# Where the weight blocks are fetched, where the first tile's FFN is placed, and which engine clears and multiplies at the start of a fused GateLoop and maxout-FFN kernel

## The chip, the cores and the metric

The kernel runs on one core of a Trainium2 chip. The metric is the device time in microseconds (us) of one execution. Five engines work side by side: TensorE (PE in the profile; PEld is its weight load), VectorE (DVE), ScalarE (ACT), GpSimd (POOL) and SyncE (SP), which issues transfers. The span that a trace shows (from the first to the last instruction) is about 1.8 us shorter than the time of the same execution.

## The reference

The reference is a gated linear recurrence over 768 steps (batch 4, 8 heads of 48), followed by a feed-forward block on its output:

```python
mag = np.sqrt(a_re * a_re + a_im * a_im)
scale = np.minimum(mag, 0.999) / (mag + 1e-06)
a_re_n, a_im_n = (a_re * scale, a_im * scale)
for t in range(S):                      # S = 768
    new_re = ar * S_re - ai * S_im      # ar, ai: the gates of step t
    new_im = ar * S_im + ai * S_re
    kv = np.einsum('bhd,bhe->bhde', k[:, :, t], v[:, :, t])
    S_re, S_im = (new_re + kv, new_im)
    y[:, :, t] = np.einsum('bhd,bhde->bhe', q[:, :, t], S_re)
# x = y as 3072 tokens x 384
h = np.maximum(np.maximum(x @ w1, x @ w2), x @ w3)     # w1..w3: 384 x 768
out = h @ w_out                                        # w_out: 768 x 384
```

The weights are made as `np.random.randn(...) * (1.0 / np.sqrt(n))` and arrive as float64, so the kernel must turn them into float32 on the chip. Everything else is float32.

## The kernel before

The 3072 tokens are 24 tiles of 128; two tiles are a group that shares one pass of gate work (logarithms, angles, products), so there are twelve groups. A tile goes through its gates, a Q and K preparation, the recurrence in chunked form, then nine "up" steps (three column blocks by w1, w2, w3, with a maximum on VectorE) and one "out" step (`op`) of the FFN. The up steps need the rounded w1 to w3, the out step needs all of w_out.

The twelve weight blocks of 768 KB are rounded like this; each takes five operations on VectorE and two on ScalarE:

```python
def load_weight(dst, src, i):
    ...
    if i % 3 == 2:
        raw = wo...                     # part of a weight tile not yet in use
    else:
        raw = fp2.tile([P, n, m, 2], I32, tag="hT", name="raw")
    nc.sync.dma_start(out=raw..., in_=src.bitcast(I32))
    low, high = raw[:, :, :, 0].bitcast(U32), raw[:, :, :, 1]
    ex = fp2.tile([P, n, m], I32, tag="xT", name="ex")
    nc.vector.tensor_scalar(out=ex, in0=high, scalar1=0x7FF00000, scalar2=None, op0=OP.bitwise_and)
    nc.scalar.activation(out=ex, in_=ex, func=AF.Relu, scale=8.0, bias=wbias)
    nc.vector.scalar_tensor_tensor(out=ex, in0=high, scalar=-0x80000000, in1=ex,
                                   op0=OP.bitwise_and, op1=OP.bitwise_or)
    nc.vector.tensor_scalar(out=high, in0=high, scalar1=0x000FFFFF, scalar2=None, op0=OP.bitwise_and)
    nc.scalar.activation(out=dst, in_=high, func=AF.Copy, scale=2.0 ** -20, bias=1.0)
    nc.vector.scalar_tensor_tensor(out=dst, in0=low, scalar=2.0 ** -52, in1=dst, op0=OP.mult, op1=OP.add)
    nc.vector.tensor_tensor(out=dst, in0=dst, in1=ex.bitcast(FP), op=OP.mult)
```

The multiplies that GpSimd takes over from VectorE (`ai` by `L` in the gates, `k` and `q` by `E` in the products) are chosen by group:

```python
(nc.gpsimd if g > 0 else nc.vector).tensor_tensor(out=ai, in0=ai, in1=L, op=OP.mult)
...
eng = nc.gpsimd if g > 0 else nc.vector
eng.tensor_tensor(out=hd(T[nm, x]), in0=E, in1=hd(T[nm, x]), op=OP.mult)
```

And the order of the program; `weave` spreads several lists of steps over the given shares of one another:

```python
load(0)                                 # all of group 0's inputs, then
load_v(0)
constants_early()
for t in us["k"] + us["q"] + fs + gs + vbs[2:]:
    nc.gpsimd.memset(t, 0.0)            # whole tiles, on GpSimd
weights = weight_steps()
...                                     # gates of group 0
for f in weights[:3]:                   # the first three blocks, fetched and rounded here
    f()
load(1)
angles(0, list(range(C)))
...
for g in range(NG):
    load_v(g + 1)
    load(g + 2)
    if g == 0:
        weave((0.0, 1.0, loop_steps(0)), (0.0, 0.7, weights[3:]),
              (0.15, 0.58, pre_steps(1)), (0.7, 1.0, ffn_steps([0])))
    else:
        ...
```

## Time and profile before

| | before |
|---|---|
| time, median of the first 3 runs | 751.53 us (751.1 to 753.01) |
| span of the profiled execution | 748.2 us |
| end of the last multiply that rounds weights ("T") | 123.24 us |
| TensorE busy / idle up to T | 59.79 / 63.45 us |
| TensorE busy / idle after T | 611.13 / 13.83 us |

The page gives the busy share of 40 slices in tenths; the table of stretches gives exact busy time between two chosen moments; the waits say who sat idle for whom; the timeline lists single instructions with start and duration. One more piece of the timeline of VectorE before the first cumulative sum (columns: start, duration, engine, line, operation, output<-inputs, size):

```profile
28.42 0.95 DVE L345 TENSOR_TENSOR w<-w,ar 128x768 f32<-128x768 f32 x1
29.29 1.82 DVE L281 SCALAR_TENSOR_TENSOR w<-raw,w 128x768 f32<-128x768 uint32 x2
31.03 1.82 DVE L282 TENSOR_TENSOR w<-w,ex 128x768 f32<-128x768 f32 x2
32.77 0.56 DVE L274 TENSOR_SCALAR ex<-wo 128x768 int32<-128x768 int32 x1
33.23 0.95 DVE L346 TENSOR_TENSOR w<-w,ai 128x768 f32<-128x768 f32 x1
```

L345 and L346 are the two angle operations that the cumulative sum needs.

### The profile page before, as it was taken

Reading aid. Unit: us, or ns where it says so; the run is one execution under the profiler, and the core shown is the slowest. Engines: PE = TensorE matmul, PEld = TensorE weight load, DVE = VectorE, ACT = ScalarE, POOL = GpSimd, SP = SyncE. Lnnn points to the kernel's source line nnn. Section 1 sums busy time; section 2 is a strip of 40 time slices with the busy share of each in tenths; the row PEclk is TensorE's granted clock in tenths of the full one; section 3 lists DMA queues with packets and bytes.
Section 4 is the critical chain, followed back from the end, with each engine's and each line's share of the span. In section 5 each row is a group of like instructions: output and inputs, shape, how many; then the busy total and the mean of one; then the engine's idle time right before and its main releaser. Section 6 shows DMA issues by size and latency. Waiting matters only on the chain.

```text
span 748.2 us, 17645 instructions
## 1 busy us (share of the span) xinstructions
PE 670.9 (90%) x7620; PEld 543.1 (73%) x7620; DVE 518.4 (69%) x706; ACT 402.2 (54%) x677; POOL 130.4 (17%) x133
## 2 busy tenths in 40 slices
PE   1166279989999999999999999999999999999998
PEld 0054168968778878878878868878878878788785
DVE  4889997787866866866856867867857767655210
ACT  7595565666647546556556556556566465322010
POOL 9302400411302203102103103103004005000000
PEclk9986699999999999999999999999999999999999
DMA  9764430050220320320320420410410210000000
GB/s 173 156 178 136 121 92 23 8 103 10 54 65 11 56 66 9 74 51 7 72 54 6 77 52 5 91 35 7 91 33 10 46 33 2 1 23 2 12 11 22
DMA packets 134158, 38.91 MB, mean 52 GB/s; under 512 B 126784, under 2 KB 129856, under 8 KB 134080
## 3 DMA queue, kind: packets, MB, share of 16 engines
q1 hardware_dynamic: 133824, 37.76, 22.8%
q8 instruction: 60, 0.98, 0.6%
q14 instruction: 18, 0.15, 0.1%
q10 hardware_dynamic: 256, 0.01, 0.0%
HBM read 33.03 MB, written 4.72 MB: 50 GB/s over the span
## 4 chain that ended last, share of the span: by engine, by line
PE 73%; issue 11%; DVE 7%; ACT 4%; POOL 2%; SPq 2%; DMA 1%; ACTq 0%; POOLq 0%; DVEq 0%
PE up L575 35%; PE op L586 12%; PE tp L432 5%; PE dk L529 4%; PE B L492 4%; PE y L557 3%; PE A L492 2%; PE mds L395 2%; PE sfx L395 2%; PE F L445 2%; PE cs L350 2%; ACT e L106 1%; DVE QB L459 1%; SPq L226 1%; POOL ai L328 1%
## 5 line engine op out<-in xcount | busy, mean ns | idle before, releaser
L575 PE MATMUL up<-xT,w 128*128 128x256 f32 (+1 forms) x1404 | 299.3, 367 | 6.5 <-ACT xT L563 6.2
L575 PEld LDWEIGHTS up<-xT,w 128*128 128x128 f32 x1404 | 249.0, 191 | 46.4 <-ACT xT L563 7.7
L328 POOL TENSOR_TENSOR ai<-ai,L 128x768 f32<-128x768 f32 x11 | 30.4, 2759 | 418.4 <-ACT L L106 314.1
L586 PE MATMUL op<-wo,hT 128*128 128x384 f32 x288 | 97.9, 490 | 0.0
L580 DVE TENSOR_TENSOR hT<-hT,up 128x512 f32<-128x512 f32 (+1 forms) x78 | 49.9, 640 | 40.0 <-PE up L575 39.8
L586 PEld LDWEIGHTS op<-wo,hT 128*128 128x128 f32 x288 | 52.9, 190 | 33.3 <-DVE hT L580 0.5
L459 DVE TENSOR_TENSOR Q<-Q,f 112x512 f32<-112x512 f32 x48 | 40.3, 840 | 44.9 <-ACT f L106 44.9
L434 ACT COPY K<-tp 112x512 f32<-112x512 f32 x48 | 27.9, 581 | 60.0 <-PE tp L432 59.8
L578 ACT COPY hT<-up 128x512 f32<-128x512 f32 (+1 forms) x39 | 21.3, 548 | 69.6 <-PE up L575 68.6
L588 ACT COPY ot<-op 128x384 f32<-128x384 f32 x24 | 11.5, 477 | 81.5 <-PE op L586 81.5
L541 DVE TENSOR_TENSOR g<-g,dk 112x384 f32<-112x384 f32 x40 | 22.1, 552 | 47.0 <-PE dk L529 46.4
L350 PE MATMUL cs<-w,upto 128*128 128x384 f32 x48 | 20.5, 555 | 34.5 <-DVE w L346 34.5
L529 PEld LDWEIGHTS dk<-vb,uk 128*112 128x112 f32 x384 | 42.7, 183 | 9.9 <-issue 5.5
L557 PEld LDWEIGHTS y<-atm,vb 128*32 128x32 f32 x1536 | 39.7, 112 | 13.5 <-issue 8.4
L529 PE MATMUL dk<-vb,uk 128*112 128x96 f32 x384 | 43.1, 267 | 6.0 <-issue 5.2
L557 PE MATMUL y<-atm,vb 128*32 128x64 f32 x1536 | 47.1, 224 | 0.4 <-DVE atm L510 0.4
L557 PE MATMUL y<-QG,g 112*32 112x64 f32 x1536 | 46.5, 222 | 0.0
L459 DVE TENSOR_TENSOR QB<-Q,f 112x512 f32<-112x512 f32 (+1 forms) x48 | 46.3, 999 | 0.0
L405 POOL TENSOR_TENSOR k<-E,k 128x384 f32<-128x384 f32 x22 | 30.2, 1372 | 68.9 <-ACT E L106 65.2
L492 PE MATMUL A<-Q,K 112*64 112x96 f32 x768 | 38.7, 254 | 3.7 <-DVE Q L459 3.1
L492 PEld LDWEIGHTS A<-Q,K 112*64 112x64 f32 x768 | 33.9, 140 | 9.4 <-issue 5.2
L106 ACT ACTIVATE f<-F 48x296 f32<-48x296 f32 x96 | 39.6, 412 | 1.7 <-PE F L445 0.4
(107 smaller groups left out, 1126.9 us busy)
## 6 DMA issues: line engine op xcount, KB each, us to landing
ar<-in_a_re_dram SPq DMA_DIRECT2D x24, 192.0 KB, 3.6
ai<-in_a_im_dram SPq DMA_DIRECT2D x24, 192.0 KB, 4.0
k<-in_k_dram SPq DMA_DIRECT2D x24, 192.0 KB, 3.0
q<-in_q_dram SPq DMA_DIRECT2D x24, 192.0 KB, 3.0
vb<-in_v_dram SPq DMA_DIRECT2D x96, 48.0 KB, 2.4
raw<-in_moe_w_dram SPq DMA_DIRECT2D x6, 768.0 KB, 5.6
out_dram<-ot SPq DMA_DIRECT2D x24, 192.0 KB, 1.9
wo<-in_moe_w_dram SPq DMA_DIRECT2D x3, 768.0 KB, 6.4
```

What stands on the lines that cost most here:

```text
L106: tab(nc.scalar.activation(**kw))
L328: (nc.gpsimd if g > 0 else nc.vector).tensor_tensor(out=ai, in0=ai, in1=L, op=OP.mult)
L350: nc.tensor.matmul(out=ps, lhsT=upto, rhs=w[:, c * DM:(c + 1) * DM], start=True, stop=c == 0)
L405: eng.tensor_tensor(out=hd(T[nm, x]), in0=E, in1=hd(T[nm, x]), op=OP.mult)
L432: nc.tensor.transpose(out=tp[0:DD, j], in_=both(T["U" + nm, x], hg * HU + j), identity=ident)
L459: nc.vector.tensor_tensor(out=out, in0=in_, in1=f.to_broadcast([DD, H, 2 * n, 8]), op=OP.mult)
L492: nc.tensor.matmul(out=ps[o:o + L64, h // HU, h % HU * 96:h % HU * 96 + 96], lhsT=K[0:DD, h, o:o + L64], rhs=Q[0:DD, 2 * h + c], start=Tru ...
L529: nc.tensor.matmul(out=ps[0:DD, h // HU, h % HU * 96:h % HU * 96 + 96], lhsT=both(T["Uk", x], h), rhs=T["v", x][:, :, h // 2, o:o + D], st ...
L557: nc.tensor.matmul(out=y[32 * (r % 4):32 * (r % 4) + 32, r // 4, c * L64:(c + 1) * L64], lhsT=V[:, c, i, lo:lo + 32] if new else G[0:DD, c ...
L575: nc.tensor.matmul(out=ps[:, j], lhsT=ws[i][:, d, f * P:(f + 1) * P], rhs=xT[:, d], start=(d == 0), stop=(d == KD - 1))
L580: nc.vector.tensor_tensor(out=dst, in0=dst, in1=ps, op=OP.max)
L586: nc.tensor.matmul(out=ps, lhsT=hT[:, f, o:o + P], rhs=wo[:, f], start=(f == 0), stop=(f == KF - 1))
```

## The change

The intent: VectorE has idle moments while the first gates wait for inputs and for ScalarE, and TensorE idles until the weights are rounded. So fetch weight blocks early enough to round them in these moments, let the first tile's FFN run while the last blocks are being rounded, clear only what must be cleared (and less of it on GpSimd), and keep GpSimd off group 1. The core of the diff:

```diff
-            (nc.gpsimd if g > 0 else nc.vector).tensor_tensor(out=ai, in0=ai, in1=L, op=OP.mult)
+            (nc.gpsimd if g > 1 else nc.vector).tensor_tensor(out=ai, in0=ai, in1=L, op=OP.mult)
...
-                eng = nc.gpsimd if g > 0 else nc.vector
+                eng = nc.gpsimd if g > 1 else nc.vector
...
-    for t in vbs[:2]:
+    for t in vbs:
         nc.gpsimd.memset(t, 0.0)
-    load(0)
-    load_v(0)
+    blocks = weight_blocks()
+    for c in range(C):
+        load_a(0, c)
+        weight_load(c)
+    load_kq(0, 0)
+    weight_load(2)
+    load_kq(0, 1)
+    load(0, load_v)
+    for i in range(3, 6):
+        weight_load(i)
+    for t in fs:
+        nc.gpsimd.memset(t[L64 // 2:L64], 0.0)
+    for t in gs:
+        nc.vector.memset(t[:, :, :, D:P - D], 0.0)
+    for t in us["k"] + us["q"]:
+        nc.vector.memset(t[:, :, 0, D:], 0.0)
     constants_early()
-    for t in us["k"] + us["q"] + fs + gs + vbs[2:]:
-        nc.gpsimd.memset(t, 0.0)
...
-            weave((0.0, 1.0, loop_steps(0)), (0.0, 0.7, weights[3:]), (0.15, 0.58, pre_steps(1)), (0.7, 1.0, ffn_steps([0])))
+    rounds = []
+    for i in range(3, len(blocks)):
+        rounds.append(call(weight_round, i))
+        if i + 4 < len(blocks):
+            rounds.append(call(weight_load, i + 4))
+    load(1, load_v, load_kq)
+    ffn = ffn_steps([0])
+    weave((0.0, 1.0, tile_steps(0) + tile_steps(1)), (0.0, 0.7, rounds), (0.15, 0.58, pre_steps(1)),
+          (0.4, 0.7, ffn[:9]), (0.72, 0.8, ffn[9:]))
```

Cut: `load_weight` is split into a fetch and a rounding, with raw data put into five different free places; the loaders are split per tile; the first tile's FFN input and hidden values go into other buffers; one mask is made later. The arithmetic of the rounding is the same.

More of the change, by code (lines that the diff above doesn't have):

```diff
@@ L156, in constants_early @@
     def constants_early():
-        keep(upto, 0, [[1, P]], -1)
         halves = mid.rearrange("p (n u h) -> p n u h", u=2, h=4)
@@ L164, in constants_early @@
         keep(right, 4, [[8, 16], [1, 4]], -1)
+        keep(upto, 0, [[1, P]], -1)
         make_identity(nc, ident)
@@ L217, in rows, with load_a, load_kq, load_v @@
         return a[b, :, t0:t0 + n, :].rearrange("h t d -> t h d")
-    def load(g):
-        if g >= NG:
-            return
+    def load_a(g, c):
         for nm, src in (("ar", a_re), ("ai", a_im)):
-            T[nm, g] = ld2.tile([P, C, H, D], FP, tag=nm, name=nm)
-        for c in range(C):
-            for nm, src in (("ar", a_re), ("ai", a_im)):
-                nc.sync.dma_start(out=T[nm, g][:, c], in_=rows(src, g, c))
-        for c in range(C):
-            x = g * C + c
-            for nm, src in (("k", k), ("q", q)):
-                T[nm, x] = ldx.tile([P, H, D], FP, tag=nm, name=nm)
-                nc.sync.dma_start(out=T[nm, x], in_=rows(src, g, c))
-    def load_v(g):
-        if g >= NG:
-            return
-        for c in range(C):
-            x = g * C + c
-            T["v", x] = vbs[x % 4]
-            for h in range(2):
-                src = rows(v, g, c, h * L64, L64).rearrange("t (i u) d -> t i u d", u=2)
-                for u in range(2):
-                    nc.sync.dma_start(out=heads(T["v", x][h * L64:(h + 1) * L64, h])[:, :, u], in_=src[:, :, u])
+            if c == 0:
+                T[nm, g] = ld2.tile([P, C, H, D], FP, tag=nm, name=nm)
+            nc.sync.dma_start(out=T[nm, g][:, c], in_=rows(src, g, c))
+    def load_kq(g, c):
+        for nm, src in (("k", k), ("q", q)):
+            t = T[nm, g * C + c] = ldx.tile([P, H, D], FP, tag=nm, name=nm)
+            nc.sync.dma_start(out=t, in_=rows(src, g, c))
+    def load_v(g, c):
+        x = g * C + c
+        T["v", x] = vbs[x % 4]
+        for h in range(2):
+            src = rows(v, g, c, h * L64, L64).rearrange("t (i u) d -> t i u d", u=2)
+            for u in range(2):
+                nc.sync.dma_start(out=heads(T["v", x][h * L64:(h + 1) * L64, h])[:, :, u], in_=src[:, :, u])
+    def load(g, *parts):
+        for part in parts if g < NG else ():
+            for c in range(C):
+                part(g, c)
     ws = [const.tile([P, KD, FF], FP, name="w%d" % i) for i in range(3)]
     wo = const.tile([P, KF, DM], FP, name="wo")
-    def weight_steps():
-        steps, n = [], FF // 3
+    def weight_blocks():
+        blocks, n = [], FF // 3
         for f in range(3):
@@ L252, in weight_steps, with weight_load @@
                 cols = slice(f * n, (f + 1) * n)
-                steps.append(call(load_weight, w[:, :, cols], src.rearrange("(i p) m -> p i m", p=P)[:, :, cols], len(steps)))
+                blocks.append((w[:, :, cols], src.rearrange("(i p) m -> p i m", p=P)[:, :, cols]))
         for f in range(0, KF, 2):
-            view = moe_w_out.rearrange("(i p) m -> p i m", p=P)
-            steps.append(call(load_weight, wo[:, f:f + 2], view[:, f:f + 2], 0))
-        return steps
-    def load_weight(dst, src, i):
+            blocks.append((wo[:, f:f + 2], moe_w_out.rearrange("(i p) m -> p i m", p=P)[:, f:f + 2]))
+        return blocks
+    def weight_load(i):
+        dst, src = blocks[i]
         if src.dtype == FP:
@@ L264, in load_weight, with weight_round @@
         n, m = dst.shape[1:]
-        if i % 3 == 2:
-            raw = wo.bitcast(I32).rearrange("p f m -> p (f m)")[:, 0:2 * n * m].rearrange("p (n m w) -> p n m w", n=n, w=2)
-        else:
-            raw = fp2.tile([P, n, m, 2], I32, tag="hT", name="raw")
-        nc.sync.dma_start(out=raw.rearrange("p n m w -> p n (m w)"), in_=src.bitcast(I32))
+        if i in (0, 1, 2, 6):
+            room = (ws[1], ws[2], wo)[i % 4].rearrange("p f m -> p (f m)")
+            room = room[:, FF // 3 * KD:].rearrange("p (n m) -> p n m", n=n)
+        elif i == 5:
+            room = un2.tile([P, n, 2 * m], FP, tag="Q", name="raw")
+        else:
+            room = fp2.tile([P, n, 2 * m], FP, tag="hT", name="raw")
+        T["raw", i] = room.bitcast(I32)
+        nc.sync.dma_start(out=T["raw", i], in_=src.bitcast(I32))
+    def weight_round(i):
+        dst, src = blocks[i]
+        if src.dtype == FP:
+            return
+        n, m = dst.shape[1:]
+        raw = T["raw", i].rearrange("p n (m w) -> p n m w", w=2)
         low, high = raw[:, :, :, 0].bitcast(U32), raw[:, :, :, 1]
@@ L560, in outputs @@
         if x == xs[0]:
-            T["xT", xs[-1]] = fp2.tile([P, KD, len(xs) * P], FP, tag="xT", padded_shape=[P, KD, TG], name="xT")
+            T["xT", xs[-1]] = fp2.tile([P, KD, P], FP, tag="ot", name="xT") if len(xs) == 1 else \
+                fp2.tile([P, KD, TG], FP, tag="xT", name="xT")
         o = (x - xs[0]) * P
@@ L568, in up_step @@
         if fp == 0 and i == 0:
-            T["hT", xs[-1]] = fp2.tile([P, KF, n], FP, tag="hT", padded_shape=[P, KF, TG], name="hT")
+            T["hT", xs[-1]] = ld2.tile([P, KF, n], FP, tag="ar", name="hT") if xs[0] == 0 else \
+                fp2.tile([P, KF, n], FP, tag="hT", padded_shape=[P, KF, TG], name="hT")
         dst = T["hT", xs[-1]][:, 2 * fp:2 * fp + 2]
@@ L613, in front, with tile_steps @@
             [call(prep, x, p) for p in range(4)]
-    def loop_steps(g):
-        steps = []
-        for x in range(g * C, (g + 1) * C):
-            tr, ct, pr = front(x + 1)
-            kt = [products(x + 1)[2]] if x + 1 < NX else []
-            steps += [call(scores, x, "A"), call(gather, x, "A"), call(scores, x, "B")] + tr[:1]
-            steps += [call(gather, x, "B"), call(state, x)] + tr[1:] + ct + pr[:1] + kt
-            steps += [call(outputs, x, tokens(x))] + pr[1:]
-        return steps
+    def tile_steps(x):
+        tr, ct, pr = front(x + 1)
+        kt = [products(x + 1)[2]] if x + 1 < NX else []
+        return [call(scores, x, "A"), call(gather, x, "A"), call(scores, x, "B")] + tr[:1] \
+            + [call(gather, x, "B"), call(state, x)] + tr[1:] + ct + pr[:1] + kt \
+            + [call(outputs, x, tokens(x))] + pr[1:]
     table("natural_log_exp_and_others")
-    for t in vbs[:2]:
+    for t in vbs:
         nc.gpsimd.memset(t, 0.0)
-    load(0)
-    load_v(0)
+    blocks = weight_blocks()
+    for c in range(C):
+        load_a(0, c)
[12 more added lines that the diff above has]
+        nc.vector.memset(t[:, :, 0, D:], 0.0)
     constants_early()
-    for t in us["k"] + us["q"] + fs + gs + vbs[2:]:
-        nc.gpsimd.memset(t, 0.0)
-    weights = weight_steps()
     for pair in zip(*(gate_steps(0, [c]) for c in range(C))):
@@ L638 @@
         products(c)[0]()
-    for f in weights[:3]:
-        f()
-    load(1)
+    for i in range(3):
+        weight_round(i)
+    weight_load(6)
+    load(1, load_a)
     angles(0, list(range(C)))
@@ L645, with feed @@
         f()
-    for g in range(NG):
-        load_v(g + 1)
-        load(g + 2)
-        if g == 0:
-            weave((0.0, 1.0, loop_steps(0)), (0.0, 0.7, weights[3:]), (0.15, 0.58, pre_steps(1)), (0.7, 1.0, ffn_steps([0])))
-        else:
-            ffn = ffn_steps(tokens(g * C - 1))
-            def feed(n):
-                for _ in range(min(n, len(ffn))):
-                    ffn.pop(0)()
-            weave((0.0, 1.0, loop_steps(g)), (0.0, 0.7, pre_steps(g + 1, feed)),
-                  (0.0, 1.0 if g > 1 else 0.5, [call(feed, 1) for _ in ffn]))
+    rounds = []
[7 more added lines that the diff above has]
+          (0.4, 0.7, ffn[:9]), (0.72, 0.8, ffn[9:]))
+    load(2, load_a, load_kq)
+    for g in range(1, NG):
+        load(g + 1, load_v)
+        load(g + 2, load_a, load_kq)
+        ffn = ffn_steps(tokens(g * C - 1))
+        def feed(n):
+            for _ in range(min(n, len(ffn))):
+                ffn.pop(0)()
+        weave((0.0, 1.0, tile_steps(g * C) + tile_steps(g * C + 1)), (0.0, 0.7, pre_steps(g + 1, feed)),
+              (0.0, 1.0 if g > 1 else 0.5, [call(feed, 1) for _ in ffn]))
     for f in ffn_steps(tokens(NX - 1)):
```

## The prediction

> **What bounds the kernel now.** I read the page first, then the busy time of each engine in stretches, then the waits and the timeline of the first 124 us. From the page, busy tenths in 40 slices of 18.7 us:
>
> ```profile
> PE   1166279989999999999999999999999999999998
> ...
> DVE  4889997787866866866856867867857767655210
> ...
> PEclk9986699999999999999999999999999999999999
> ```
>
> From slice 7 on TensorE is full to the end; in the first six slices it is not, and there VectorE is the full one. The borders are instructions I picked in the timeline: 5.48 us is VectorE's first gate operation, 34.20 us the first cumulative sum on TensorE, 49.08 us the first Q preparation, 123.24 us the end of the last multiply that rounds a weight block. Columns are stretch, length, then busy us and instruction count of PE, PEld, DVE, ACT, POOL, then granted clock, DMA share and GB/s:
>
> ```profile
> 5.48:34.20 28.72, 3.27 (x4) 1.00 (x4) 20.76 (x37) 20.11 (x36) 18.84 (x49) 1.00 0.85 174
> 34.20:49.08 14.88, 10.24 (x48) 7.15 (x48) 11.82 (x17) 11.39 (x22) 0.00 (x0) 0.77 0.87 217
> 49.08:70.98 21.90, 13.65 (x216) 11.26 (x220) 21.90 (x32) 16.37 (x25) 0.00 (x1) 0.70 0.41 133
> 70.98:82.30 11.32, 2.93 (x66) 2.10 (x54) 9.63 (x10) 5.87 (x9) 9.34 (x5) 0.80 0.32 87
> 82.30:123.24 40.94, 29.71 (x355) 25.67 (x356) 39.79 (x58) 22.05 (x36) 2.18 (x1) 0.80 0.36 83
> ...
> 0.00:123.24 123.24, 59.79 (x677) 47.19 (x678) 104.79 (x160) 78.11 (x127) 35.21 (x73) 0.83 0.55 132
> 123.24:748.20 624.96, 611.13 (x6945) 495.91 (x6944) 413.64 (x547) 324.09 (x550) 95.14 (x60) 1.00 0.17 36
> ```
>
> Up to 123.24 us TensorE does 59.79 us of work and idles 63.45; after it, it idles 13.83 of 624.96 us. So the end is set by **when VectorE has rounded the float64 weights** (call it T, 123.24 now) and by how much TensorE has left at T. After 49.08 us VectorE idles only 2.84 us up to T, before it 15.6. The groups in the waits and the timeline that the change aims at:
>
> ```profile
> PE cs L350 <- DVE w L346: 33.0, 2, 18.8
> ...
> DVE w L330 <- POOL ai L328: 1.7, 1, 1.7
> ```
>
> ```profile
> 70.98 4.59 POOL L328 TENSOR_TENSOR ai<-ai,L 128x768 f32<-128x768 f32 x1 [45.76 <-ACT L L106]
> ...
> 75.60 1.73 DVE L330 SCALAR_TENSOR_TENSOR w<-w,ai 128x768 f32<-128x768 f32 x1 [1.69 <-POOL ai L328]
> 77.26 1.74 DVE L282 TENSOR_TENSOR w<-w,ex 128x768 f32<-128x768 f32 x1
> 78.93 1.75 DVE L418 TENSOR_TENSOR uk<-uk,En 128x768 f32<-128x768 f32 x1
> 80.59 1.74 DVE L276 SCALAR_TENSOR_TENSOR ex<-raw,ex 128x768 int32<-128x768 int32 x1
> ```
>
> VectorE waits 1.69 us for a GpSimd multiply, and four operations that take 0.95 us elsewhere take 1.74 while GpSimd multiplies.
>
> **What the Trainium skill says.** SBUF — State Buffer, "Who interferes with whom": a VectorE instruction with two SBUF inputs contends with a GpSimd instruction that reads SBUF, not with one that only writes it. The trace agrees (0.95 becomes 1.74 us above). DMA: Bandwidth & Descriptors, "Why small descriptors are slow": each packet has a fixed overhead. The trace agrees: the first gate inputs, 192 KB each in runs of 48 floats, follow each other about 1.05 us apart (ScalarE starts on them at 3.88, 4.92, 5.97 and 7.01 us); a 768 KB weight block lands 4.3 us after issue at best. TensorE: Matmul & The Clock Gate, "HAM oscillation": idle gaps put the array back to half clock. The trace agrees, 0.70 to 0.80 in the stretches with gaps and 1.00 after; but while VectorE is the bound a faster clock there moves nothing. Perfetto Trace Analysis, "Optimization Strategy": regimes with different bounds gain from being interleaved. That is the intent here.
>
> **The change, part by part.** Steady cost on VectorE, start to start: 0.87 us for 128x768 with two inputs, 0.47 with one, 0.47 for 128x384, 1.13 for 112x1024, 0.60 for 112x512, 0.35 for a max of 128x256. One block's rounding is 0.47+0.87+0.47+0.87+0.87 = 3.55, twelve blocks 42.6 us, neither added nor removed. I took each engine's order from the built kernel.
>
> *1. Weights fetched between the first inputs, rounded between the gates.* Start to 34.2 us. The queue now holds a 768 KB block before the second chunk's gate inputs. If it moves in about 2.4 us (estimate: the 4.3 us less the 1.9 us in which the 1.5 KB carry row lands), block 0 is there at 7.4 us, the second chunk's inputs at 9.5, blocks 1 and 2 at 12 and 16.5. VectorE fills waits with rounding, but ScalarE, which ran the gates nearly without a gap to 21.3 us, gets two exponent passes and two conversions (0.9 us each) ahead of its table load, so that load goes to about 25.5. Then Arctan, and only 3.6 us of VectorE work instead of the present queue (25.2 to 34.2): the cumulative sum starts at **30.5, not 34.2: 3.7 us**.
>
> *2. From there to the Q preparation* VectorE now has blocks 3 and 4 at hand while it waits for sines, 14 us of work in a stretch of 14.9, of which I let 1.3 be lost again, for ScalarE has two more passes there: the stretch takes 16.2. Q preparation at 46.7, with more already done: of block 3 two operations (1.75), block 4 four (3.1), block 5 one (0.47), less group 1's first two gate operations (1.35), not done yet: 3.9 us ahead.
>
> *3. Constants first.* Seven short VectorE clears (about 1.2 us, estimate from 0.17 us for 128x128) fall before the first input lands; 26 us of GpSimd clears shrink to a few. Of VectorE's waits there only 1.7 us (for the masks, at 25 us) are charged to GpSimd, and those lie before the cumulative sum counted in step 1. On top of step 1: 0.
>
> *4. Group 1 without GpSimd.* Adds 0.87 + 4 x 0.47 = 2.75 us to VectorE, takes away 4 x 0.79 = 3.2 plus 0.3 on the next ones, and the 1.69 us wait. Net 2.4 us.
>
> *5. First tile's FFN beside the rounding.* Nine up steps (1.5 us each warm, 2.9 cold) and the out step (4.0) move no work off VectorE: two more maxima fall before T (+0.7), and the present order does Q/K preparation of tile 2 (KB, two QB, QG, one uk: 1.13+0.60+1.13+1.13+0.87 = 4.9) before T, the new one after it. TensorE at T: now the whole out step (4.04) is left; then only its last third (1.35) and 0.7 us of tile 2's scores that are now done before. **2.0 us less left at T.**
>
> *Sum for T.* Work after Q preparation now: 123.24 - 49.08 - 2.84 = 71.3. New: 71.3 - 3.9 + 2.75 + 0.7 - 4.9 - 3.5 = 62.5. T = 46.7 + 62.5 = 109.2 plus stalls. Stalls now 2.84, of which 1.69 goes; but the new order has VectorE waiting for TensorE's maxima right behind the cumulative sum (about 1.5), and raw buffers for w_out are reused two deep, so blocks 10 and 11 are fetched only when 8 and 9 are done, with 4.4 to 4.6 us of VectorE work to cover a landing of at least 4.3, behind k and q (2 to 3). I put stalls at 4.5: **T = 113.7, 9.5 us earlier**. Then TensorE: 624.96 - 2.0, plus 0.7 because VectorE brings 4.9 us of preparation into the stretch after T (13.5 of 20 us busy from 120 to 140 now, 18 then). Span 113.7 + 623.7 = 737.4, against 748.2: **10.8 us**. 751.5 - 10.8 = 740.7, rounded to 741.
>
> **The rivals.** (a) *The early gates are held up by the weights in the queue.* For it: DMA is 85% busy from 5.48 to 34.2 us, ScalarE's chain starts from those inputs, and extra passes sit in it. Against: that chain's result then waited about 9 us behind rounding on VectorE. If the cumulative sum starts at 34 as now, 3.7 us are lost: 744. (b) *TensorE becomes the bound before T.* For it: nine up steps at 2.9 us cold are 26 us in a stretch of some 35 us of VectorE work. Against: when dense they warm to 1.5. It would cost 3 to 5 us: 744 to 746. (c) *VectorE never stalls after 46.7*: T = 109.2, span 733, time 736. (d) *The gain is given back later*: group 2's ar now waits for a buffer that group 1 frees, its first tile's hT sits in a buffer that group 3's ar needs. The trace has those loads land in about 4 us with far more slack, so I give it little; it would make "same" by 1 to 3 us less.
>
> **Range and chances.** Two per cent is 15 us, 736.5; only (c) with a better start reaches it. Slower by 15 us would need new stalls of 26 us, which nothing shows. Range 735 to 746; faster 0.17, same 0.81, slower 0.02.
>
> **What would show each step.** First cumulative sum near 30.5 us (step 1), first Q preparation near 46.7 (2), no 1.7 us VectorE operation near 75 us and no GpSimd multiply before group 2 (4), last w_out multiply near 114 us (sum), TensorE idle falling from 77 to about 66 us, with nearly all the fall before T, and after T no more than 15 us. The prediction fails if T falls below 109 (more waits filled than I think), if the first sum starts at 34 or later, or if TensorE's idle after T grows by over 3 us.

## The result, and the profile after

The changed kernel took **743.25 us** (median of 4 runs, 741.61 to 744.82), the kernel before beside it 751.41 (4 runs). Ratios are the mean time of one kernel's fast runs over that of the other's of the same rounds, so not quite the ratio of the medians: here 0.9887, 95% interval 0.9858 to 0.9916. That is 1.1% less, within 2%, and the time lies in the predicted range, 2.3 us above the predicted value.

The page after, slices of 18.5 us, the rows that answer to those of before:

```profile
PE   1266779789999999999999999999999999999998
DVE  5999998897857867767757767767767677565210
PEclk9687799999999999999999999999999999999999
```

TensorE's digits of 6 and 7 now come in slices 3 to 6 and VectorE is at 8 or 9 in all of slices 2 to 8. The stretches between the same landmarks as before (first gate operation, first cumulative sum, first Q preparation, T); the columns are as in the prediction's table:

```profile
5.55:31.79 26.24, 3.27 (x4) 1.01 (x4) 22.14 (x36) 19.63 (x36) 14.51 (x43) 0.83 0.85 223
31.79:48.18 16.39, 10.84 (x48) 7.34 (x48) 14.43 (x24) 12.82 (x23) 2.88 (x9) 0.64 0.96 179
48.18:113.32 65.14, 46.18 (x622) 37.51 (x620) 63.12 (x94) 42.36 (x66) 1.03 (x1) 0.82 0.36 93
...
0.00:113.32 113.32, 60.29 (x672) 45.85 (x672) 101.83 (x169) 77.13 (x127) 23.32 (x61) 0.80 0.58 139
113.32:740.50 627.18, 609.95 (x6952) 494.97 (x6949) 419.34 (x550) 323.65 (x550) 93.76 (x60) 1.00 0.18 37
```

T is 113.32 us, 9.9 earlier. Up to T TensorE does what it did before (60.29 us) and idles 53.03 instead of 63.45. The span falls by only 7.7 us (748.2 to 740.5): **TensorE's idle time after T rises from 13.83 to 17.23 us**, 3.4 us. The waits of TensorE between 113 and 200 us show one entry that the kernel before has not (total, times, longest):

```profile
PE op L600 <- DVE hT L594: 3.4, 1, 3.4
```

In the timeline of that place (GpSimd's multiply, VectorE's operations behind it, then TensorE's out step):

```profile
129.28 2.59 POOL L338 TENSOR_TENSOR ai<-ai,L 128x768 f32<-128x768 f32 x1 [55.70 <-ACT L L106]
...
131.90 1.76 DVE L340 SCALAR_TENSOR_TENSOR w<-w,ai 128x768 f32<-128x768 f32 x1 [1.37 <-POOL ai L338]
...
133.58 1.50 DVE L469 TENSOR_TENSOR Q<-Q,f 112x512 f32<-112x512 f32 x1
135.01 2.02 DVE L469 TENSOR_TENSOR KB<-K,f 112x1024 f32<-112x1024 f32 x1
...
140.97 2.01 DVE L469 TENSOR_TENSOR QG<-Q,f 112x1024 f32<-112x1024 f32 x1
...
143.71 0.41 DVE L594 TENSOR_TENSOR hT<-hT,up 128x256 f32<-128x256 f32 x1
...
144.17 1.56 PE L600 MATMUL op<-wo,hT 128*128 128x384 f32 x4 [3.41 <-DVE hT L594]
```

The out step of tile 1 waits for the last maximum (143.71), which stands on VectorE behind group 2's gate operations. Group 2 is now the first group whose multiplies run on GpSimd, and it meets VectorE with little slack right behind T: VectorE first waits 1.37 us for GpSimd's multiply, then five operations of it (those above and one QB) take 8.8 us where they take 4.7 in a_g2v below, which has group 2's multiplies on VectorE (0.95, 0.68, 1.21, 0.68, 1.21 us).

### The profile page after: what moved, and what is told of

It reads as the page before. It is cut to its first block, busy times and chain, and to the rows that moved or that the text cites. A ratio compares the mean times of both kernels' runs of the same rounds, so it can differ in the third digit from the quotient of the medians.

```text
span 740.5 us, 17637 instructions
## 1 busy us (share of the span) xinstructions
PE 670.2 (91%) x7620; PEld 540.8 (73%) x7620; DVE 521.2 (70%) x718; ACT 400.8 (54%) x677; POOL 117.1 (16%) x121
## 4 chain that ended last, share of the span: by engine, by line
PE 71%; issue 13%; DVE 7%; ACT 6%; DMA 1%; POOL 1%; SPq 0%; ACTq 0%; POOLq 0%; DVEq 0%
PE up L589 34%; PE op L600 12%; PE tp L442 5%; PE dk L539 4%; PE B L502 4%; PE y L567 3%; PE A L502 3%; ACT e L106 2%; PE mds L405 2%; PE cs L360 2%; PE sfx L405 2%; PE F L455 2%; ACT L L106 1%; ACT w L106 1%; PE cs L362 1%
## 5 line engine op out<-in xcount | busy, mean ns | idle before, releaser
L338 POOL TENSOR_TENSOR ai<-ai,L 128x768 f32<-128x768 f32 x10 | 25.8, 2578 | 382.4 <-ACT L L106 309.0
L502 PE MATMUL B<-QB,KB 112*64 112x96 f32 x768 | 37.8, 252 | 7.3 <-DVE QB L469 7.3
L502 PEld LDWEIGHTS B<-QB,KB 112*64 112x64 f32 x768 | 33.8, 140 | 11.5 <-issue 10.9
L405 PE MATMUL mds<-Ln,mid 128*128 128x384 f32 x48 | 23.9, 582 | 20.1 <-POOL cuts L120 15.9
```

The costliest lines, as they stand in the source:

```text
L338: (nc.gpsimd if g > 1 else nc.vector).tensor_tensor(out=ai, in0=ai, in1=L, op=OP.mult)
L405: nc.tensor.matmul(out=ps, lhsT=mat, rhs=T["Ln", g][:, c * DM:(c + 1) * DM], start=True, stop=True)
L502: nc.tensor.matmul(out=ps[o:o + L64, h // HU, h % HU * 96:h % HU * 96 + 96], lhsT=K[0:DD, h, o:o + L64], rhs=Q[0:DD, 2 * h + c], start=Tru ...
```

## The experiments

Every kernel gave the right result and was timed in 5 rounds with the kernel before on the same chip. The runs came in three calls on two chips; call 1 has a control, the changed kernel itself. To compare I use the ratio to before, times 751.4 us. The half widths of the differences are estimates: those of the two ratios, added in squares.

| kernel | median us (lowest to highest, runs) | ratio to before, 95% | us against after |
|---|---|---|---|
| a_same (control) | 743.61 (742.11 to 744.82, 6) | 0.9889 (0.9867 to 0.9911) | 0 |
| a_wlate | 752.69 (748.64 to 754.16, 6) | 1.0004 (0.9979 to 1.0029) | +8.6 ± 2.5 |
| a_clears | 747.14 (746.82 to 747.94, 6) | 0.9949 (0.9933 to 0.9965) | +4.5 ± 2.0 |
| a_g1p | 748.74 (746.8 to 750.77, 6) | 0.9958 (0.9932 to 0.9984) | +5.2 ± 2.6 |
| a_ffnlate | 745.3 (742.7 to 747.7, 6) | 0.9909 (0.9883 to 0.9935) | +1.5 ± 2.6 |
| a_f35 | 744.69 (743.35 to 745.69, 5) | 0.9912 (0.9895 to 0.993) | +1.7 ± 2.1 |
| a_g2v | 739.22 (738.97 to 740.37, 4) | 0.9843 (0.9825 to 0.9861) | -3.5 ± 2.1 |
| a_nogp | 737.62 (737.15 to 738.57, 5) | 0.9819 (0.9803 to 0.9835) | -5.3 ± 2.0 |
| a_bits | 734.07 (733.05 to 734.26, 4) | 0.9769 (0.9751 to 0.9786) | -9.0 ± 2.1 |
| a_bits_g2v | 728.86 (727.07 to 730.04, 4) | 0.9700 (0.968 to 0.972) | -14.2 ± 2.2 |
| b_g1v | 748.53 (747.79 to 749.45, 6) | 0.9965 (0.995 to 0.9981) | (-2.6 ± 1.2 against before) |
| b_wearly | 758.49 (751.06 to 759.35, 7) | 1.0099 (1.0082 to 1.0116) | (+7.4 ± 1.3 against before) |

Kernels whose names begin with a start from the changed kernel, those with b from the kernel before.

### The control (a_same)

> The changed kernel once more, as the control for the three kernels beside it. 743.3 us, within 1.5 us of the first measurement; ratio to before 0.989. In its profile the last w_out multiply ends near 113.3 us and TensorE waits once, about 3.4 us, for the last hT maximum of tile 1 near 141 to 144 us. If that wait is an accident of one execution and not of the order, it is absent here.

The median is 743.61 us; T is 112.41 in its trace and the wait of the out step is there again, so what I read in the first trace was no accident. One caution comes from it. After T its TensorE is busy 612.50 us where the first trace of the same kernel has 609.95, at a granted clock of 0.99 instead of 1.00. Two executions of one kernel differ by 2.6 us in this term, so a difference of 1 or 2 us in it, such as the one that I forecast, can't be read off one trace.

### The weights fetched behind the inputs (a_wlate)

```diff
-    for c in range(C):
-        load_a(0, c)
-        weight_load(c)
-    load_kq(0, 0)
-    weight_load(2)
-    load_kq(0, 1)
-    load(0, load_v)
-    for i in range(3, 6):
+    load(0, load_a, load_kq, load_v)
+    for i in range(6):
         weight_load(i)
```

> The changed kernel with all inputs of group 0 fetched before the first weight block, as before the change; the rounding stays where the program has it. Theory (the early blocks fill VectorE's waits): first cumulative sum back to 34 us, Q preparation near 49 with less rounded by then, end of rounding 4 to 6 us later, time 4 to 6 us over the control. Rival (the weights in the queue delay the gates as much as they help): first cumulative sum no later than the control's 31.8 us, time within 1.5 us of the control.

The whole gain is gone (+8.6 us), more than the 4 to 6 that I expected. The reason is not the one I gave. The first cumulative sum of a_wlate on TensorE, with VectorE's operation L356 as releaser:

```profile
30.43 2.93 PE L360 MATMUL cs<-w,upto 128*128 128x384 f32 x4 [14.94 <-DVE w L356]
```

In the control it starts at 30.79. The early fetch makes the sum no earlier at all. What it buys is seen in the stretch from the first gate operation to that sum, a_wlate first, then the control:

```profile
5.54:30.43 24.89, 3.27 (x4) 1.00 (x4) 16.94 (x34) 18.39 (x34) 13.14 (x51) 1.00 1.05 263
```

```profile
5.60:30.79 25.19, 3.27 (x5) 1.00 (x5) 21.85 (x36) 19.60 (x36) 14.99 (x42) 1.00 0.87 231
```

VectorE is busy 16.94 us in a_wlate and 21.85 in the control: 4.9 us more of work, with 14 finished rounding operations in place of 7, is done in moments in which VectorE otherwise waits, mostly for ScalarE. It is not free: ScalarE's arctangent, from which VectorE computes the angles, starts at 26.55 us in the control and at 24.01 in a_wlate. But less VectorE work stands between it and the sum, and so the sum is only 0.4 us later. The work not done early comes back: from the first Q preparation (45.02 in a_wlate, 46.81 in the control) to T, VectorE is busy 69.13 us against 63.11 and waits 5.6 against 2.5. T is 119.70 in a_wlate, 7.3 us later than in the control. Its profiled execution (748.64 us) was the fastest of six, the others took 752.5 to 754.2; what those 4 us are is not in any trace and stays open. (The record lists a granted clock of 0.964 to 0.973 for them and 0.976 for the profiled one; whether that is the cause is not shown.)

### Only the early fetch, in the kernel before (b_wearly)

The first three blocks go between the first inputs as in the changed kernel; all else is as before.

```diff
-    load(0)
+    for c in range(C):
+        for nm, src in (("ar", a_re), ("ai", a_im)):
+            nc.sync.dma_start(out=T[nm, 0][:, c], in_=rows(src, 0, c))
+        early(c)                        # fetch of block c
+    kq0(0)
+    early(2)
+    kq0(1)
...
-    for f in weights[:3]:
-        f()
+    for i in range(3):
+        rounded(first[i][0], raws[i], KD, FF // 3)
```

> The kernel before with nothing but the first three weight blocks fetched between the first inputs, each into the buffer it had. Theory (early blocks fill VectorE's waits): VectorE idle from 5.5 us to the first Q preparation falls from 11 to about 6 us, end of rounding 3 to 5 us earlier, time 3 to 5 us less, ratio 0.994 to 0.996. Rival (the gain of the early fetch needs blocks 3 to 5 at hand too, which this kernel still fetches late): the first cumulative sum comes 3 us earlier but Q preparation and the end of rounding gain under 1.5 us, ratio 0.998 or more.

It is slower than before by 7.4 us. A clear miss: the part whose removal costs the changed kernel 8.6 us harms the kernel before. The trace suggests a reason. VectorE's rounding now meets GpSimd's clears, which in the kernel before stand beside waits and two-input gate operations that they do not slow (0.55 or 0.56 us each from 11.00 to 17.93 us; timeline of b_wearly: VectorE, then GpSimd):

```profile
13.45 2.31 DVE L281 TENSOR_SCALAR ex<-raw 128x768 int32<-128x768 int32 x1
```

```profile
13.52 1.83 POOL L659 MEMSET uk<- 128x1024 f32 x2
```

The operation takes 2.31 us where it takes 0.56 elsewhere, and ends 0.4 us after the two clears (15.35). So I formed a theory: early weights and small clears belong together. But the trace shows little of the price: the sum starts at 33.23 us, 1.0 earlier than before, and T is 124.72, 1.5 later. The profiled execution was again the fastest (751.06 us, no slower than the kernel before; the other six took 757.6 to 759.4), so the 7 us stay open. Nor is this edit the exact opposite of a_wlate: the changed kernel also has blocks 3 to 5 fetched ahead, and the rival of the expectation, that the early fetch needs them, is not tested; neither is the kernel before with both the early fetch and the small clears.

### The old clears in the changed kernel (a_clears)

```diff
+    constants_early()
+    for t in us["k"] + us["q"] + fs + gs:
+        nc.gpsimd.memset(t, 0.0)
-    for t in fs:
-        nc.gpsimd.memset(t[L64 // 2:L64], 0.0)
-    for t in gs:
-        nc.vector.memset(t[:, :, :, D:P - D], 0.0)
-    for t in us["k"] + us["q"]:
-        nc.vector.memset(t[:, :, 0, D:], 0.0)
-    constants_early()
```

> The kernel after with the old clears put back: constants_early first, then GpSimd clears the whole of us, fs and gs. The prediction's step 3 put the new clears at 0 (within 1 us). My theory from b_wearly (GpSimd clears slow the single-input rounding operations that now stand in the first waits) expects 2 to 5 us slower than the kernel after: first cumulative sum or Q preparation later, single-input operations of 1.1 to 2.3 us before 30 us where the kernel after has 0.4 to 0.6.

(The four `vb` tiles are still cleared first, as in the changed kernel.) It costs 4.5 us, as the theory expected (2 to 5), with all six runs within 1.2 us of one another. The timeline of a_clears, VectorE and then GpSimd:

```profile
16.61 5.43 DVE L284 TENSOR_SCALAR ex<-wo 128x768 int32<-128x768 int32 x1
21.96 0.67 DVE L338 TENSOR_TENSOR ai<-ai,L 128x384 f32<-128x384 f32 x1
```

```profile
15.15 1.84 POOL L652 MEMSET uk<- 128x1024 f32 x2
16.93 1.84 POOL L652 MEMSET uq<- 128x1024 f32 x2
18.72 1.12 POOL L652 MEMSET f<- 128x592 f32 x2
19.78 1.85 POOL L652 MEMSET g<- 128x1024 f32 x2
```

And the same instruction in the control:

```profile
16.81 0.56 DVE L284 TENSOR_SCALAR ex<-wo 128x768 int32<-128x768 int32 x1
```

One single-input operation takes 5.43 us instead of 0.56: it stands still until the row of clears has ended (21.6 us). The gate operations queue behind it, the cumulative sum comes at 35.10 instead of 30.79, and T at 116.56 instead of 112.41. The Trainium skill names this: SBUF — State Buffer, "Who interferes with whom", says that a VectorE operation in a two-port mode and a GpSimd operation contend for a shared pair of ports, that the one that issues first holds it for its whole instruction and that the other fully blocks; VectorE: DVE Perf Modes, "Mode 2×_2P", says that single-source operations on SBUF can enter such a mode. This trace agrees in both: single-input operations run at 0.47 us from start to start where two-input ones of the same size need 0.87, and it is the single-input one that stood still. It stood still for more than one instruction: the rest of one clear and six whole ones.

### Group 1 back on GpSimd (a_g1p), and group 1 off GpSimd in the kernel before (b_g1v)

```diff
-            (nc.gpsimd if g > 1 else nc.vector).tensor_tensor(out=ai, in0=ai, in1=L, op=OP.mult)
+            (nc.gpsimd if g > 0 else nc.vector).tensor_tensor(out=ai, in0=ai, in1=L, op=OP.mult)
...
-                eng = nc.gpsimd if g > 1 else nc.vector
+                eng = nc.gpsimd if g > 0 else nc.vector
```

This is a_g1p; b_g1v is the opposite edit in the kernel before.

> The changed kernel with group 1's three multiplies back on GpSimd. Theory (VectorE's work and waits before the end of the rounding set the time): the slowed VectorE operations (1.74 us for 0.95) and a wait of about 1.7 us come back, the 2.75 us of multiplies leave VectorE, net end of rounding 2.4 us later, time about 2.4 us over the control. Rival (these waits are filled by other rounding work in the new order): end of rounding within 1 us of the control's, time within 1 us.

> The kernel before with nothing but group 1's three multiplies moved from GpSimd to VectorE. Theory (VectorE's busy time and waits before the end of the rounding set the end): 4 us of slowed operations and a 1.7 us wait go, 2.75 us of work comes; end of rounding 2.4 to 4 us earlier than 123.2, time 2 to 4 us less than before, ratio 0.995 to 0.997. Rival (the undone part in the changed kernel cost 5 us only because of that kernel's order): ratio 0.998 or more.

In the kernel before the part is worth 2.6 us, near the 2.4 that I had worked out; T in its trace is 121.55, 1.7 us earlier, a little less than the 2.4 to 4 expected. In the changed kernel it is worth 5.2 (± 2.6, so the two values may yet be the same). The trace of a_g1p (its execution took 750.65 us) has T at 118.73, 6.3 us later than the control, and these operations while GpSimd works:

```profile
71.22 1.73 DVE L340 SCALAR_TENSOR_TENSOR w<-w,ai 128x768 f32<-128x768 f32 x1 [1.69 <-POOL ai L338]
72.87 1.75 DVE L428 TENSOR_TENSOR uk<-uk,En 128x768 f32<-128x768 f32 x1
...
75.48 3.40 DVE L469 TENSOR_TENSOR QB<-Q,f 112x512 f32<-112x512 f32 x1
```

The first two are the pattern that I knew from before; the third, 3.40 us where 0.68 is usual, overlaps three GpSimd operations in a row (75.38 to 78.32 us) and is new. But the slowed operations are not what makes T so late. 1.3 us of the 6.3 come before the first Q preparation (48.09 against 46.81; in the changed kernel's first trace it is 48.18). From there to T, VectorE is busy only 0.6 us longer than in the control (63.75 against 63.11), about what the forecast has; its waits are 4.4 us longer (6.9 against 2.5): 1.7 for GpSimd's multiply, as forecast, 1.7 for a ScalarE pass of the rounding at 113.43 us, and 1.0 for the maxima. Six runs of a_g1p fall into two clusters, 746.8 to 747.1 and 750.4 to 750.8: how the two engines meet seems to differ from run to run, which I can't show beyond this one trace.

### Group 2 off GpSimd too (a_g2v), and no group on it (a_nogp)

```diff
-            (nc.gpsimd if g > 1 else nc.vector).tensor_tensor(out=ai, in0=ai, in1=L, op=OP.mult)
+            (nc.gpsimd if g > 2 else nc.vector).tensor_tensor(out=ai, in0=ai, in1=L, op=OP.mult)
...
-                eng = nc.gpsimd if g > 1 else nc.vector
+                eng = nc.gpsimd if g > 2 else nc.vector
```

a_nogp has 99 in place of 2.

> The changed kernel with group 2's three multiplies on VectorE as well. Theory (GpSimd slows VectorE's five operations by 4.0 us and makes it wait 1.4 us just after the rounding, so that tile 1's last hT maximum is late and TensorE waits 3.4 us): the TensorE wait near 141 us falls under 1 us, time 2 to 3.4 us under the changed kernel's 743.4, ratio to before about 0.985. Rival (VectorE is simply behind by the work put off until after the rounding, and 2.75 us more only adds to it): the wait stays at 3 us or grows, ratio 0.989 or more.

> The kernel after with no multiply on GpSimd in any group. Group 2 alone gave 3.4 us. Behind about 200 us TensorE idles almost nowhere, so the theory that only group 2's place (right behind T) mattered expects the time of a_g2v within 1.5 us (739 plus or minus 1.5). If contention costs everywhere, another 2 to 4 us come off; if VectorE becomes too full, it is slower than a_g2v by over 2 us.

a_g2v takes back the loss behind T: 3.5 us less than the changed kernel. Its stretches (the border, 112.10, lies 0.07 before T), and two of the operations that were slowed:

```profile
0.00:112.10 112.10, 60.19 (x671) 45.84 (x672) 100.98 (x169) 77.21 (x127) 23.46 (x61) 0.80 0.58 140
112.10:737.20 625.10, 610.22 (x6954) 495.42 (x6950) 418.66 (x556) 323.16 (x550) 86.02 (x55) 1.00 0.18 37
```

```profile
130.16 0.95 DVE L340 SCALAR_TENSOR_TENSOR w<-w,ai 128x768 f32<-128x768 f32 x1
131.03 0.68 DVE L469 TENSOR_TENSOR Q<-Q,f 112x512 f32<-112x512 f32 x1
```

T is close to that of the control (112.17 and 112.41), TensorE idles 14.88 us after it instead of 17.09, and the wait of the out step is gone from the list. The edit removes both VectorE's wait for GpSimd (1.37 us) and the slowing of its operations (8.8 less 4.7, 4.1 us); it does not say which of them counts for how much. GpSimd's one-row subtraction of the carry (1x384) stays on GpSimd in every version, and beside it VectorE's `uk` still takes 1.75 us in a_g2v. Taking all groups off GpSimd gives another 1.8 us by the ratios (1.6 by the medians), TensorE's idle after T is 13.24; the intervals of the two overlap, so most of it (3.5 of 5.3 us) lies in group 2, and whether the other nine groups add anything stays open. VectorE has room for the work: after T it is busy 412.50 us of 623.10 in a_nogp. That is less than the 419.23 of the control, though it executes some 50 instructions more: behind T, GpSimd's help costs VectorE more time than it takes off it.

### The first tile's FFN late again (a_ffnlate), and tile 1's FFN earlier (a_f35)

```diff
-          (0.4, 0.7, ffn[:9]), (0.72, 0.8, ffn[9:]))
+          (0.7, 1.0, ffn))
```

> The changed kernel with the first tile's FFN woven in at 0.7 to 1.0 of group 0, as before the change. Theory: end of rounding within 1.5 us of the control's 113.3, but two to three up steps and the out step are then left to TensorE after it, so 2 to 4 us over the control. Rival (VectorE's order alone sets the time, and TensorE's gaps do not count): within 1 us of the control.

a_ffnlate is 1.5 us slower, within its error of 2.6. Its T is 114.10, 1.7 us later than in the control. Inconclusive: this part is worth little, and I can't say whether it is worth anything.

a_f35 tests whether the wait behind T is a matter of order: tile 1's FFN steps are woven into the first 35% of group 1 in place of 50%, so that the maximum comes earlier.

```diff
-              (0.0, 1.0 if g > 1 else 0.5, [call(feed, 1) for _ in ffn]))
+              (0.0, 1.0 if g > 1 else 0.35, [call(feed, 1) for _ in ffn]))
```

> The changed kernel with tile 1's FFN steps woven into the first 35% of group 1 instead of the first half, so that its last hT maxima stand before the KB, QB and QG work of the next tile in VectorE's order; GpSimd as in the changed kernel. If the wait is one of order, TensorE's 3.4 us wait goes although the slowed operations stay, ratio about 0.985. If being behind on VectorE is what costs, TensorE waits as long for the scores or the outputs of the next tile instead, ratio 0.988 or more.

The wait of the out step is gone, but in its place, in the waits of a_f35 between 113 and 200 us, stands:

```profile
PE tp L442 <- DVE uk L420: 3.7, 1, 3.7
```

and the time is no better (+1.7 ± 2.1). VectorE is behind at that moment; this reordering only changed which TensorE step waits for it. Together with a_g2v this speaks for time that VectorE loses to GpSimd as the cause, and against the order of the steps.

### Rounding with less VectorE work (a_bits), and both (a_bits_g2v)

Does T set the end, as the prediction has it, or does TensorE bound the stretch before T (its rival (b))? Here each block is put together by four bit operations on VectorE, two with one input and two with two (2.68 us where 3.55 were needed), and none on ScalarE. It cuts the mantissa instead of rounding it; the relative error is under 2^-23 by a calculation, and a weight that is exactly zero would come out wrong, which the inputs here don't have. As an experiment it gives the right result within the tolerance.

```diff
-        nc.vector.tensor_scalar(out=ex, in0=high, scalar1=0x7FF00000, ...)
-        nc.scalar.activation(out=ex, in_=ex, func=AF.Relu, scale=8.0, bias=wbias)
-        ...                             # three more on VectorE, one on ScalarE, as above
-        nc.vector.tensor_tensor(out=dst, in0=dst, in1=ex.bitcast(FP), op=OP.mult)
+        nc.vector.tensor_scalar(out=ex, in0=high, scalar1=3, scalar2=0x7FFFFFFF,
+                                op0=OP.logical_shift_left, op1=OP.bitwise_and)
+        nc.vector.tensor_scalar(out=high, in0=high, scalar1=-0x80000000, scalar2=0x40000000,
+                                op0=OP.bitwise_and, op1=OP.bitwise_xor)
+        nc.vector.scalar_tensor_tensor(out=ex, in0=low, scalar=29, in1=ex,
+                                       op0=OP.logical_shift_right, op1=OP.bitwise_or)
+        nc.vector.tensor_tensor(out=dst.bitcast(I32), in0=ex, in1=high, op=OP.bitwise_xor)
```

> The kernel after with each block rounded by four VectorE bit operations and no ScalarE pass (2.68 us of VectorE work for 3.55, so about 10.4 us less VectorE and 21.6 us less ScalarE work before the last weight multiply). If VectorE's rounding sets that moment (T) and T sets the end, the time falls by 6 to 10 us. If TensorE already bounds the stretch before T, or the waits take it back, by less than 3 us. The result is cut to 24 bits instead of rounded; the difference is below the tolerance.

> Both: bit operations, and group 2 without GpSimd as in a_g2v (which took 3.4 us off the kernel after). If the two gains lie in different stretches (before T, and behind T) they add up: 9 to 13 us under the kernel after. If the bit operations alone already leave VectorE slack behind T, group 2's change adds less than 1.5 us to a_bits.

a_bits takes 9.0 us off. Its stretches:

```profile
0.00:99.06 99.06, 55.73 (x558) 42.50 (x562) 86.93 (x153) 56.64 (x101) 30.32 (x61) 0.90 0.65 158
99.06:731.30 632.24, 614.49 (x7077) 498.60 (x7066) 421.80 (x555) 324.59 (x553) 94.81 (x60) 0.99 0.17 37
```

T is 99.06, 13.3 us earlier, more than the 10.4 us of VectorE work removed: VectorE is busy 14.5 us less up to T (86.93 against 101.47 in the control), so about 4 us of other work have moved behind T. The edit also takes 21.6 us of work off ScalarE, but that is not what brings T forward: VectorE idles no less up to T (12.1 us, 10.9 in the control). TensorE's work moves behind T in part (55.73 us before T, 59.49 in the control), so the span falls by 10.7 us against the control. TensorE's own work was not what held T. Its idle time after T is 17.75, the same loss behind T. With group 2 off GpSimd it is 14.59 and the time is **728.86 us**, 14.2 us less than the changed kernel; the sum of the two parts, 12.5, lies within the error of 2.2. This is the fastest version: 3.0% less than before, 1.9% less than the changed kernel.

## Why the prediction was right or wrong

The time, the range and the class came out right, and T (113.7 forecast, 113.32 and 112.41 measured) within 1.3 us. The path to it was partly luck: in the first trace three errors cancel (the Q preparation came 1.5 us later than forecast, VectorE's work from there was 0.6 us longer, its stalls 2.5 us shorter). And one of the prediction's own signs of failure came true: TensorE's idle after T grew by over 3 us (point 6), so its total idle fell only to 70.3 us, not to 66.

1. *Weights between the first inputs.* The number was near (cumulative sum at 30.5; measured 31.84 and 30.79), and so were its parts in the control: ScalarE's table load at 25.26 us (25.5 forecast), then 3.4 us from the arctangent's end to the sum (3.6 forecast). The step that fails is the claim that the early fetch brings the sum from 34.2 to 30.5. With the weights late the sum starts at 30.43. What held it at 34.2 was the row of rounding operations between the two angle operations (shown above); in a_wlate only one stands there. The early fetch is worth more than the forecast, for another reason: 4.9 us more of work done in VectorE's waits, and 8.6 us of time.
2. *Up to the Q preparation.* Forecast 46.7, measured 48.18 in the first trace and 46.81 in the control; in the first the first weight block also reached VectorE later (8.26 us against 7.31 in the control). The order of size was right: VectorE's work left from there to T was forecast at 62.5 and measured at 63.12. (The 3.9 us in that step's sum should be 4.0.)
3. *Constants, put at 0.* Wrong. I took the clears as something to wait for (masks, 1.7 us) and asked what they hold up as a producer. a_clears shows that they hold up VectorE's single-input operations as a neighbour: 4.5 us. The trace before had a sign of it: the single-input operation at 20.75 us takes 1.01 us beside a GpSimd clear (20.36 to 21.34), the next one, at 22.95 us, 0.56. I had read the very section that says so, but applied to this place only its sentence on two inputs.
4. *Group 1 without GpSimd, 2.4 us.* Right in the kernel before (2.6). In the changed kernel 5.2 ± 2.6: if it is more there, the term that was too small is the waits. The sum has 1.69 us of them, the trace of a_g1p 4.4; VectorE's busy time is near the forecast.
5. *FFN beside the rounding.* VectorE's stalls up to T, put at 4.5 us, measured 2.0 (65.14 less 63.12; 2.5 in the control). TensorE's work left at T, 2.0 us less: the traces have 1.2 less and 1.4 more, and can't decide it. a_ffnlate gives this part at most a small worth.
6. *After T.* Forecast +0.7 us of TensorE's idle. It grew by 3.4 (3.3 in the control). The step that fails is that I added VectorE's work behind T at its undisturbed durations; group 2's multiplies on GpSimd now fall into that crowd. Group 2 off GpSimd takes 3.5 us back (a_g2v).

Two readings under the skill's name were weaker than the prediction says. The stretch from 5.48 to 34.20 us has the largest gap (TensorE idles 25.45 of 28.72 us) and yet lists a clock of 1.00, so "0.70 to 0.80 in the stretches with gaps" leaves one out. And the spacing of 1.05 us of the 192 KB loads beside the 4.3 us from issue to landing of a 768 KB block compares two different things; it does not show an overhead of each packet. No term of the sum rests on either reading.

Rival (a), gates held up by the weights, holds for the gates (the arctangent is 2.5 us later in the control than in a_wlate) and not for the sum: it is 0.4 us later with the weights in the control, 1.4 in the first trace, and does not start at 34. Rival (b), TensorE as the bound, is ruled out by a_bits. Rival (c), no stalls, came half true (2.0 us of stalls). Rival (d), gain given back later, came true by 3.4 us, but through contention behind T, not through a load that waits for a buffer.

The span's sum, measured in the first trace: T -9.9, TensorE's work after T -1.2, its idle after T +3.4, together -7.7. And the parts are not independent: undone one by one they cost 8.6 + 4.5 + 5.2 + 1.5 = 19.8 us, of a gain of 8.3. The early fetch alone, in the kernel before, is a loss (b_wearly). What is left open: the timed executions of a_wlate and b_wearly that are 4 and 7 us slower than the profiled ones, and with the first of them about 4 of the 8.6 us that the early fetch is worth in the changed kernel.

## What to carry to other kernels

When a change brings VectorE work into moments in which it used to wait, look at what GpSimd does in those moments: clears and multiplies that were free become the cost, and a single-input operation can stand still for a whole row of clears (once here, 5.43 us for 0.56). Take GpSimd's helping multiplies out of the stretch where VectorE sets the pace and of the next one behind it, for a gain brought forward lands on whatever comes first there. And test a bundle of changes from both ends, one part undone and one part alone: an undone part may show a worth that it has only together with another.

## What the Trainium skill lacked or had wrong

- SBUF — State Buffer, "Who interferes with whom", had the rule right; it gives two factors of slowing, without the operations that they belong to, and says that a lock lasts one instruction, not what happens when GpSimd's instructions follow each other closely. Here: a two-input VectorE operation beside GpSimd multiplies goes from 0.95 us to between 1.73 and 1.76, from 1.21 to 2.0, from 0.68 to 1.50 and once to 3.40; a single-input one beside GpSimd clears from 0.56 to 2.31 and once, through a row of them, to 5.43.
- The same section says that GpSimd can be the one that blocks; I found no page that says what a row of small GpSimd operations loses. Here the same row of fourteen small selects took 2.29 us in the kernel before (7.94 to 10.23), while VectorE was mostly idle, and 5.65 in b_wearly (7.93 to 13.58), while it rounded.
- Perfetto Trace Analysis, "Optimization Strategy", advises to interleave regimes with different bounds, which held here; that section doesn't say that the interleaved work must be costed beside its new neighbours (a_clears, +4.5 us), though the page warns elsewhere, under "Optimizing Scalar/DVE Operations", that moving work between VectorE and GpSimd may not help.
- I found no page that says by how much TensorE's busy time differs between executions of one kernel: 609.95 and 612.50 us after T here.
